# One attention block: the opening reordered, the bound's rows placed apart from Q's, and small products cut into quarters of 32 columns

## The chip, the cores and the metric

The kernel runs on one core of one Trainium2 chip. A core has five engines that each work off their own queue of instructions: TensorE (PE, matrix products), VectorE (DVE), ScalarE (ACT), GpSimd (POOL) and SyncE (SP, which here only starts DMAs). The metric is the time of one execution on the device in microseconds (us); less is better. [...]

## The reference

```python
B, S, D, H = 1, 2048, 448, 16          # Dh = 28, bf16
qkv = (x @ wqkv).reshape(B, S, 3, H, Dh).transpose(2, 0, 3, 1, 4)
q, k, v = qkv[0], qkv[1], qkv[2]
scores = einsum("bhqd,bhkd->bhqk", q, k) * Dh ** -0.5
p = softmax(scores, axis=-1)
o = einsum("bhqk,bhkd->bhqd", p, v)
out = o.transpose(0, 2, 1, 3).reshape(B, S, D) @ wo
```

It is self-attention over 2048 tokens with 16 heads of 28 channels, a projection before it and one behind it. The main work is 16 x 2048 x 2048 exponentials.

## The kernel before

**Tiling.** The 16 heads form G = 4 groups of HG = 4; each head has a strip of HP = 32 partitions, 28 of channels and four for other use. Queries come in NQC = 4 chunks of QW = 512, keys in NKT = 16 tiles of 128. A *set* is one head group and one query chunk; there are 16 sets of 4 x 16 *steps*, a step being the scores of one head, one key tile and one chunk: 128 keys x 512 queries, 1024 steps in all.

**Two ways to the exponential.** ScalarE takes two steps at a time from a pair of PSUM banks, a0 or a1, and writes exp to a tile pt (do_exp, L864, 128 x 1024). VectorE takes the other steps one by one from the banks d0, d1 and at times m: it adds a bias to the scaled scores and writes int16 whose bits, read as bf16, are a rough exponential (do_a, L879, tile I, four steps of 512 columns to a tile). Two further integer additions over the whole tile (do_add, L902, tiles J, 128 x 2048) give shifted copies. The three terms are weighted through V: VA is V, and VS holds V times two constants. So a step of VectorE is one I, half a J and three products with V, a step of ScalarE half an exponential and one product.

**Scores and P·V.** The scores of a step are one product with 32 rows (L678; 64 rows when a half of the strips is alone), and products in different row strips run together. P·V writes the 32 output columns of one head (L962), so four heads fill the four column quarters of PE together: a *wave*. The softmax sum comes from a column of ones in V. When a set ends, VectorE copies its bank (o_sb, L991), DMAs gather the sums, VectorE inverts them (L1000), DMAs spread them (L1005, L1010), and POOL multiplies (L1013).

**The bound.** In place of a row maximum, the kernel subtracts a bound: norm of the query times the largest norm of a key. It sits in spare rows of the strips, as rows of the query tiles QP against ones in K. Norms are products of squared tiles with masks (L314, L369, L449, L477); the root is a halving of the exponent bits.

**The opening.** The input is transposed by PE (L573), copied to XT by ScalarE and VectorE (L581, L579), and K of the first head group is projected and its norms taken (k_first), while Q of the first set is projected (q_job) and its norm taken (qn_first). VectorE takes the maximum of K's norms (kp, L374), multiplies the root of the bound into QA and adds Q (L463). The first scores read QA directly, 32 rows each (L678, `QA,KA`). Meanwhile SP copies QA to the tiles QP (rows_first, L613), behind 16 loads of a constant (L176); from then on scores read QP. V is projected per half of the groups and pair of key tiles (v_job, L513, full products of 224 columns) and scaled (vs_job, L532).

**What sets the order.** No engine's order is written by hand. A planner in the kernel's code runs at build time: it keeps a clock per engine (`free`), the time at which each value is there (`evt`) and each PSUM bank is free (`res`), and asks in turn each engine what it issues next (pick_pe, pick_act, pick_dve and so on). Jobs are entered with `add`, with a duration, what they need and give, the bank they take and a priority. Scores go first when their bank is free; then P·V waves, small jobs and, to keep PE in use, products of zeros (`dense`), as long as they end before the next scores are due (`s_deadline`). d_more gives VectorE a step when it would be done in time (`dve_ok`). The durations are constants:

```python
LATS = {("ACT", "PE"): 0.32, ("PE", "ACT"): 0.12, ("PE", "DVE"): 0.15, ("DVE", "PE"): 0.2}
D_S = 0.325
D_WAVE = 0.2135
D_SWITCH = 0.11
D_EXP = 0.912
SLOW_V = 1.03
```

On the chip only the order counts that comes out of this, and the semaphores between engines.

**The end.** Behind the last exponential the last set is normalised by small products instead of DMAs (L1196, L1203) and its output projected (L1213), with early parts of that projection (early_jobs, L1146) placed between (`filler`).

## Time and profile before

| | us |
|---|---|
| median of three runs | 370.25 (370.12 to 370.31) |
| the profiled execution | 370.24 |
| its span, first to last instruction | 368.4 |
| ScalarE busy, 384 instructions | 350.4 |
| of this the exponentials, L864, 368 of them | 339.2 |
| VectorE busy, 632 instructions | 347.3 |
| of this I, L879 (260 from d, 28 from m) | 170.1 and 19.0 |
| of this J, L902, 144 of them | 102.5 |
| PE busy (matmuls) | 349.5 |
| POOL busy | 72.7 |

Times in the rows below are microseconds from the start of the span. A row of a timeline gives start, length, engine, line, operation, output <- inputs, shapes, and the idle time before it with what ended it; instructions that follow each other are merged as xN. PE's matmuls overlap, so a busy PE is not a PE at its peak: the distance from start to start is what counts. The granted TensorE clock was 0.999 throughout.

### The profile page before, as it was taken

The page shows a single profiled execution, that of the slowest core. Times are in us where ns is not written, and L with a number is a line of the kernel's source. Part 1 is how long each engine was busy: PE and PEld are TensorE (multiplying, and loading weights), DVE is VectorE, ACT ScalarE, POOL GpSimd, SP SyncE. Part 2 cuts the span into 40 slices and gives each one's busy share as a digit, 9 for nine tenths or more (in the row PEclk, how much of TensorE's full clock was granted, in tenths as well). Part 3 has the DMA queues.
Part 4 walks back from the last instruction along what each step waited for, and adds up shares of the span by engine and source line. Part 5 has one row for each costly group of instructions (what it writes and reads, how often), then busy time and mean ns, then how long its engine had stood idle before and what let it go on. Part 6 is the DMA issues. An engine that isn't in the chain of part 4 may idle for free.

```text
span 368.4 us, 8926 instructions
## 1 busy us (share of the span) xinstructions
PE 349.5 (95%) x3522; PEld 111.6 (30%) x3522; DVE 347.3 (94%) x632; ACT 350.4 (95%) x384; POOL 72.7 (20%) x95
## 2 busy tenths in 40 slices
PE   8899999999999999999999999998898999999995
PEld 4443322222333233232222222222222222222222
DVE  7799999998999999999999999999999999999973
ACT  4599999999999999999999999999999999999991
POOL 8931033242010511221011314201010101010010
PEclk9999999999999999999999999999999999999999
DMA  8510010011001000010000002100000001010101
GB/s 254 126 39 12 3 29 31 8 41 36 6 29 32 2 4 28 22 52 16 29 3 9 23 4 59 24 16 18 24 8 10 25 27 55 26 56 27 42 16 50
DMA packets 15058, 12.18 MB, mean 33 GB/s; under 512 B 6812, under 2 KB 13096, under 8 KB 15016
## 3 DMA queue, kind: packets, MB, share of 16 engines
q1 hardware_dynamic: 13464, 10.19, 9.7%
q10 hardware_dynamic: 1040, 1.02, 0.9%
q8 instruction: 27, 0.44, 0.5%
q0 software_dynamic: 512, 0.40, 0.5%
q14 instruction: 15, 0.12, 0.1%
HBM read 7.58 MB, written 1.96 MB: 26 GB/s over the span
## 4 chain that ended last, share of the span: by engine, by line
PE 52%; ACT 30%; DVE 10%; issue 6%; DVEq 0%; ACTq 0%
ACT pt L864 30%; PE a L678 19%; PE o L962 16%; PE m L270 7%; DVE I L879 4%; DVE J L902 4%; PE m L547 1%; PE m L513 1%; PE o L595 1%; PE o L708 1%; PE d L678 1%; PE m L314 1%; DVE osb L552 1%; PE d L573 1%; PE a L270 1%
## 5 line engine op out<-in xcount | busy, mean ns | idle before, releaser
L864 ACT ACTIVATE pt<-a 128x1024 bf16<-128x1024 f32 x368 | 339.2, 1125 | 1.1 <-PE a L678 0.4
L879 DVE TENSOR_SCALAR I<-d 128x512 int16<-128x512 f32 x260 | 170.1, 682 | 5.3 <-PE d L678 3.9
L678 PE MATMUL a<-QP,KA 32*128 32x512 bf16 (+1 forms) x726 | 141.6, 381 | 11.2 <-ACT pt L864 10.1
L962 PE MATMUL o<-pt,VA 128*32 128x512 bf16 x736 | 105.5, 385 | 0.0
L902 DVE TENSOR_SCALAR J<-I 128x2048 int16<-128x2048 int16 x144 | 102.5, 744 | 0.2
L678 PEld LDWEIGHTS <-KA 32*128 32x128 bf16 (+1 forms) x1024 | 48.5, 91 | 145.4 <-issue 144.5
L678 PE MATMUL d<-QP,KA 32*128 32x512 bf16 x256 | 84.0, 384 | 0.4 <-DVE I L879 0.3
L962 PE MATMUL o<-J,VS 128*32 128x512 bf16 x576 | 78.7, 385 | 0.4 <-DVE J L902 0.4
L962 PE MATMUL o<-I,VA 128*32 128x512 bf16 x288 | 66.3, 386 | 0.1
L1013 POOL TENSOR_TENSOR xs<-o_sb,rr 128x512 bf16<-128x512 f32 x12 | 16.6, 1382 | 103.3 <-DMA rr<-scr 87.0
L962 PEld LDWEIGHTS <-VA 128*32 128x32 bf16 x1024 | 24.2, 94 | 36.7 <-issue 36.3
L280 POOL TENSOR_TENSOR sq<-QA 128x512 bf16<-128x512 bf16 x15 | 18.3, 1219 | 60.9 <-DVE QA L420 60.9
L270 PE MATMUL m<-XT,WRAW 112*32 112x512 bf16 x384 | 29.5, 384 | 0.0
L280 POOL TENSOR_TENSOR sq<-KA 128x512 bf16<-128x512 bf16 x12 | 13.2, 1102 | 59.2 <-DVE KA L298 59.2
L962 PEld LDWEIGHTS <-VS 128*32 128x32 bf16 x576 | 18.1, 94 | 19.7 <-issue 19.7
L879 DVE TENSOR_SCALAR I<-m 128x512 int16<-128x512 f32 x28 | 19.0, 679 | 0.1
L513 PE MATMUL m<-WRAW,XT 112*128 112x224 bf16 x128 | 17.1, 261 | 0.2
L1013 POOL TENSOR_TENSOR OTL<-o_sb,rr 128x512 bf16<-128x512 f32 x3 | 4.1, 1367 | 56.3 <-DMA rr<-scr 56.3
L708 PE MATMUL o<-zero 128*128 128x512 bf16 x40 | 13.5, 386 | 0.0
L513 PEld LDWEIGHTS <-XT 112*128 112x128 bf16 x128 | 10.2, 97 | 7.1 <-issue 7.1
L991 DVE COPY o_sb<-o 128x512 f32<-128x512 f32 x15 | 10.3, 684 | 1.4 <-PE o L962 1.3
L547 PE MATMUL m<-WO,xs 128*128 128x448 bf16 x36 | 10.9, 358 | 0.3 <-DVE I L879 0.2
(119 smaller groups left out, 195.8 us busy)
## 6 DMA issues: line engine op xcount, KB each, us to landing
rr<-scr SPq DMA_DIRECT2D x15, 256.0 KB
QP<-QA SPq DMA_DIRECT2D x60, 28.0 KB
out_dram<-osb SPq DMA_DIRECT2D x12, 112.0 KB
WRAW<-in_wqkv_dram SPq DMA_DIRECT2D x3, 392.0 KB
xs<-in_x_dram ACTq DMA_DIRECT2D x4, 224.0 KB
xs<-in_x_dram SPq DMA_DIRECT2D x4, 224.0 KB
QP<-su SPq DMA_DIRECT2D x30, 2.0 KB
out_dram<-VS SPq DMA_DIRECT2D x2, 224.0 KB
```

The lines of the kernel that those rows point to most:

```text
L270: nc.tensor.matmul(out=ps[HP * i:HP * (i + 1), :], lhsT=w[:, cc, h * Dh:h * Dh + HP], rhs=XT[c][cc // 2][:, cc % 2, :], start=(cc == 0), s ...
L280: nc.gpsimd.tensor_tensor(out=t[:], in0=src, in1=src, op=ALU.mult)
L513: nc.tensor.matmul(out=held[key][:, part * w:(part + 1) * w], lhsT=XT[b][cc // 2][:, cc % 2, t * P:(t + 1) * P], rhs=WRAW[2][:, cc, h * w: ...
L547: nc.tensor.matmul(out=held[key][:, 0:D], lhsT=otile(g, c)[:, tq * P:(tq + 1) * P], rhs=WO[:, g, :], start=(g == 0), stop=(g == G - 1))
L678: nc.tensor.matmul(out=out_ap, lhsT=KAt[(g, j // XB)][r, (j % XB) * P:(j % XB + 1) * P], rhs=q[r, :], start=True, stop=True, tile_position ...
L708: nc.tensor.matmul(out=cur["o"][:], lhsT=zero[:, 0:P], rhs=zero[:], start=False, stop=False, skip_group_check=True)
L864: nc.scalar.activation(out=pt[:], in_=ps[:], func=ACT.Exp, scale=LN2 / 128.0)
L879: nc.vector.tensor_scalar(out=dst, in0=pd[:], scalar1=BIAS, scalar2=0.0, op0=ALU.add, op1=ALU.max)
L902: nc.vector.tensor_scalar(out=r[:, w], in0=ch["I"][:, w], scalar1=float(SHIFT[k]), scalar2=None, op0=ALU.add)
L962: nc.tensor.matmul(out=o[HP * i:HP * (i + 1), :], lhsT=vt[:, j % XB, gg, HP * i:HP * (i + 1)], rhs=e["ap"], start=(SETMM[key] == 1), stop= ...
L991: nc.vector.tensor_copy(out=st["o_sb"][:], in_=o[:])
L1013: nc.gpsimd.tensor_tensor(out=otile(g, c), in0=st["o_sb"][:], in1=st["rr"][:], op=ALU.mult)
```

## The change

- **The bound of the first set.** It is no longer added to Q. Q's tile qt goes to QP by DMA as soon as it is copied (28 rows each), the bound is scaled on its own into the tile su and placed by two more DMAs. Until both have landed, scores are two products in the same bank: one of qt and one of su. The root of the query's norm is taken from PSUM on VectorE in fp32; the copy on ScalarE (L454) is gone. The margin sits in blockK.
- **The opening's banks and engines.** K's quarters and Q use other PSUM banks; two of the four copies of K (second and third quarter) are made by ScalarE; copies wait for the squares.
- **V.** It is projected for head group 0 alone, then for group 1 alone, then for groups 2 and 3 together; tiles and scalings are split alike. The gates of the later parts change.
- **Quarters.** Norm products beyond the first set, V's projection, the output projection and the zero products into an open bank are issued as four products of 32 output columns each (`quarters`).
- **The planner's costs.** D_SWITCH becomes D_TURN, charged when scores follow column work; latencies and durations change; the factor 1.03 on VectorE goes; waves are chosen one at a time.
- **The end.** The last set's scratch uses other tiles, and one filler product stands earlier.

The diff, cut to what the prediction speaks of:

```diff
-LATS = {("ACT", "PE"): 0.32, ("PE", "ACT"): 0.12, ("PE", "DVE"): 0.15, ("DVE", "PE"): 0.2}
-D_S = 0.325
-D_WAVE = 0.2135
-D_SWITCH = 0.11
-D_EXP = 0.912
-SLOW_V = 1.03
+LATS = {("ACT", "PE"): 0.165, ("PE", "ACT"): 0.167, ("PE", "DVE"): 0.13, ("DVE", "PE"): 0.145}
+D_S = 0.323
+D_TURN = 0.143
+D_WAVE = 0.226
+D_EXP = 0.904
+TOL = 0.1
...
-S_LEAD = 0.44
+S_LEAD = 0.49
...
+    def quarters(out, lhsT, rhs, start, stop, **k):
+        for i in range(P // HP):
+            r = slice(HP * i, HP * (i + 1))
+            nc.tensor.matmul(out=out[r, :], lhsT=lhsT[:, r], rhs=rhs, start=start, stop=stop, tile_position=(0, HP * i), **k)
...
-            nc.tensor.matmul(out=held[key][:, 0:QW], lhsT=maskK[:, sc, :], rhs=sqt.pop(("K", g, sc))[:],
-                             start=(sc == 0), stop=(sc == NQC - 1))
+            quarters(held[key][:, 0:QW], maskK[:, sc, :], sqt.pop(("K", g, sc))[:], sc == 0, sc == NQC - 1)
...
         def scaled():
-            held["z0"] = wk.tile([P, QW], BF16, name="z", bufs=1)
-            nc.scalar.mul(out=held["z0"][:], in_=held.pop("qn0")[:, 0:QW], mul=MARG ** 4)
...
-        def join():
-            QAt[(0, 0)] = big.tile([P, QW], BF16, name="QA0", tag="QA0", bufs=1)
-            nc.vector.scalar_tensor_tensor(out=QAt[(0, 0)][:], in0=held.pop("nq")[:], scalar=held.pop("kroot")[:, 0:1],
-                                           in1=qtt.pop(0)[:], op0=ALU.mult, op1=ALU.add)
+            su = held["su0"] = wk.tile([P, QW], BF16, name="su", bufs=1)
+            nc.vector.tensor_scalar(out=su[:], in0=held.pop("nq"), scalar1=held.pop("kroot")[:, 0:1], scalar2=None,
+                                    op0=ALU.mult)
+
+        def place():
+            for k in range(2):
+                r = slice(HP * k + Dh, P, 2 * HP)
+                nc.sync.dma_start(out=QP[0][k][0][r, :], in_=held["su0"][r, :])
...
-            q = QP[c][i % 2][g % 2] if w else QAt[(0, 0)]
...
-            nc.tensor.matmul(out=out_ap, lhsT=KAt[(g, j // XB)][r, (j % XB) * P:(j % XB + 1) * P], rhs=q[r, :],
-                             start=True, stop=True, tile_position=(r.start, 0))
+            terms = [QP[c][i % 2][g % 2]] if w else [qtt[0], held["su0"]]
+            for n, q in enumerate(terms):
+                nc.tensor.matmul(out=out_ap, lhsT=KAt[(g, j // XB)][r, (j % XB) * P:(j % XB + 1) * P], rhs=q[r, :],
+                                 start=(n == 0), stop=(n == len(terms) - 1), tile_position=(r.start, 0))
...
+            for u in range(part * n // 2, (part + 1) * n // 2):
+                for cc in range(CC):
+                    quarters(held[key][:, u * w:(u + 1) * w], XT[b][cc // 2][:, cc % 2, (t0 + u) * P:(t0 + u + 1) * P],
+                             WRAW[2][:, cc, g0 * HG * Dh:g1 * HG * Dh], cc == 0, cc == CC - 1)
...
-    k_first(1, "a1", None, "DVE", "ACT", 2.5)
-    k_first(2, "d1", "a0", "DVE", "ACT", 3.2, late=True)
-    k_first(3, "o", "m", "DVE", "ACT", 3.3, late=True)
-    q_job(0, 0, "d0", QPRI, split=1)
-    qn_first("a1", 3.5)
+    k_first(1, "a1", "o", "ACT", "ACT", 3.05, late=("ksq", 0, NQC - 1))
+    k_first(2, "d0", "a0", "ACT", "ACT", 3.1, late=("ksq", 0, NQC - 1))
+    k_first(3, "d1", "o", "DVE", "ACT", 3.2, late=("QA", 0, 0))
+    q_job(0, 0, "m", QPRI, split=1)
+    qn_first("a0", 3.3)
...
-            r = slice(HP * i, HP * (i + 1))
-            nc.sync.dma_start(out=QP[0][i % 2][0][r, :], in_=QAt[(0, 0)][r, :])
...
+            r = slice(HP * i, HP * i + Dh)
+            nc.sync.dma_start(out=QP[0][i % 2][0][r, :], in_=qtt[0][r, :])
...
+    for b in range(NXB):
+        v_job(1, b, 0, "m", 50 + b, STEPS + 10 + 12 * b)
+        vs_job(1, b, 60 + b)
+    a, z = 2 * STEPS, 2 * NQC * STEPS - 30
```

## The prediction

> **What bounds the kernel now.** I read the busy times first, then the chain of waits, the busy time of one long stretch, and the timelines of PE, DVE and POOL at single places.

> ```profile
> PE 349.5 (95%) x3522; PEld 111.6 (30%) x3522; DVE 347.3 (94%) x632; ACT 350.4 (95%) x384; POOL 72.7 (20%) x95
> ```

> Three engines are near full, so no share alone names the limit. The chain in order of time (start, length) gives ScalarE's floor:

> ```profile
> 30.80 0.76 ACT pt L864
> ...
> 31.70 0.77 ACT pt L864
> ...
> 32.61 0.78 ACT pt L864
> ...
> 33.51 0.79 ACT pt L864
> ```

> One exponential starts every 0.904 us. There are 368, the first at 19.08 and the last at 358.79: 367 steps at 0.904 are 331.8, the stretch is 339.7, so ScalarE loses 7.9. The busy time of VectorE from its first I to its last J (columns: window, length, busy):

> ```profile
> 19.96:356.70 336.74, 328.14 (x553) 1.00 0.08 24
> ```

> VectorE has only 8.6 idle in 336.7: it is nearly as full as ScalarE. Then what makes ScalarE lose. First, matmuls of unlike shape in one visit (PE timeline):

> ```profile
> 88.08 0.61 PE L962 MATMUL o<-pt,VA 128*32 128x512 bf16 x6
> 88.62 0.39 PE L477 MATMUL m<-sq,maskK 128*128 128x512 bf16 x1
> 88.94 0.39 PE L678 MATMUL a<-QP,KA 32*128 32x512 bf16 x2
> ...
> 89.27 0.39 PE L477 MATMUL m<-sq,maskK 128*128 128x512 bf16 x1
> 89.59 0.40 PE L962 MATMUL o<-J,VS 128*32 128x512 bf16 x4
> ```

> Each change between column quarters (128*32), full products (128*128) and scores (32*128) comes 0.32 after the one before; two quarter groups of one visit start 0.217 apart (150.70 and 150.93 below). A change of shape thus costs about 0.095. Here five visits fill 1.84 (88.08 to 89.92, the next scores), where two periods of ScalarE hold 1.81, and the exponential after 88.24 comes 0.29 late. Second, POOL under VectorE's J (rows of the DVE and the POOL timeline):

> ```profile
> 60.77 1.75 DVE L902 TENSOR_SCALAR J<-I 128x2048 int16<-128x2048 int16 x1
> ```

> ```profile
> 60.70 1.27 POOL L1013 TENSOR_TENSOR xs<-o_sb,rr 128x512 bf16<-128x512 f32 x1 [1.56 <-DMA rr<-scr]
> ```

> J takes 0.68 in most cases, 1.75 here. Twelve J of 144 are stretched so, 10 us in all. By start times, ScalarE has 43 gaps over 0.93; some 1.8 of its loss stand behind a stretched J, some 4.5 behind a PE that works without a pause, the rest in the first rounds.

> **The change, part by part.** Sums are made against the profiled execution, 370.24 (span 368.4 and 1.8 around it), which is the median, 370.25, within 0.01.

> *First scores.* Before, the bound is joined to Q by QA L463 (0.75) and the scores start behind it (rows of the DVE and of the PE timeline: start, length):

> ```profile
> 16.67 0.69 DVE L374 TENSOR_REDUCE kp<-m 128x1 f32<-128x512 f32 x1
> 17.28 0.28 DVE L458 TENSOR_SCALAR su<-z 128x512 int16<-128x512 int16 x1
> 17.48 0.15 DVE L378 TENSOR_REDUCE kmt<-kp 128x1 f32<-128x4 f32 x1
> 17.66 0.15 DVE L380 TENSOR_SCALAR kroot<-kmt 128x1 int32<-128x1 int32 x1
> 17.85 0.75 DVE L463 SCALAR_TENSOR_TENSOR QA<-su,kroot,qt 128x512 bf16<-128x512 bf16 x1
> ```

> ```profile
> 18.66 0.39 PE L678 MATMUL a<-QA,KA 32*128 32x512 bf16 x2 [0.32 <-DVE QA L463]
> ```

> After, the last maximum still starts near 16.6: the square of K's last quarter is still the third on ScalarE behind its projection, and that is still PE's last (moved behind one norm product). Then kmt, kroot and the scaled rows. No row has that scale (512 fp32 to bf16): between 0.21 (su's pace) and 0.60 (a copy of 512 fp32); I take 0.34, nearer the first as it reads no PSUM. The rows are ready at about 18.0. But ahead of the scores PE now makes V of a whole token block, 16 groups of four quarters of 112 columns. No row shows such a group. From below, 224 columns take 0.095 (L513 starts) and so 112 take 0.049; from above, fp32 quarters of 128 columns take 0.46 for 16, so 0.115 for four:

> ```profile
> 362.38 0.64 PE L1203 MATMUL a<-identf,rT 128*32 128x128 f32 x16
> 362.84 0.62 PE L1203 MATMUL o<-identf,rT 128*32 128x128 f32 x16
> ```

> I take 0.065, near the lower end, because bf16 quarters keep the pace of a full product (0.217 for 512). V then ends near 17.55, a filler and the first q product follow, and the first bound product starts at 18.18. The exponential needs 0.64 more (a second pair of slots, then 0.42 as from 18.66 to 19.08): 18.8 for 19.08, a gain of 0.3.

> *Rounds two to six.* Until the query rows are placed by DMA, each score is two products in the same 32 rows, the second behind the first. A round of three scores holds four slots of 0.217, for one or two before. PE's order has, from the second round to the seventh: 19 score slots (4.12), ten changes of shape (0.95), three fillers and one wave of P·V (0.87), four V halves of eight groups (2.08 at 0.065): 8.0, and 0.65 from the first bound product to round two. The seventh exponential, the first from placed rows, starts at 18.18 + 0.65 + 8.0 + 0.42 = 27.2; before, the seventh starts at 25.36 (two rows of 0.904 behind 23.55). **+1.9** with the first gain inside. By 0.049 per group it is +1.2, by 0.115 +4.3. Nothing hides it: ScalarE has no other work there, and one V copy left on it for three (0.41 each) lies ahead of the first exponential.

> *The rows' DMAs.* That Q's rows go alone lets them start when Q is copied (near 15.8), but SP works off the 16 loads of offs until then:

> ```profile
> 7.37 11.10 SPq L176 DMA_DIRECT2D QP<-offs  x16
> 18.63 2.48 SPq L613 DMA_DIRECT2D QP<-QA  x4
> ```

> They start at 18.5 as before, now four of 28 rows (0.82 apart at L425) and two of the bound (0.59 apart): issued by 22.5, landed by about 24.1 (1.6 behind the issue, as the packets of L613). PE comes to the first wide round at 26.8, so they cost nothing; behind them SP has only the next Q's rows, due after 30.

> *Two exponentials fewer.* The planner now gives 366 to ScalarE and 292 half steps to VectorE (before 288): 2 x 0.904 = **-1.8**.

> *Quarters and the planner's new costs.* Pricing each group in PE's order by 0.217 for 512 columns and 0.095 for a change of shape, the part of a round above 0.904, summed over rounds 24 to 345, falls from 4.2 to 2.9 (741 changes of shape become 685 over all). The 4.5 that ScalarE loses to a busy PE fall by the same share: **-1.5**. Bounds: nothing, and -3.0 if short overfull rounds are caught by the buffers.

> *VectorE.* It gains four I (0.60 each), two J (0.60), two V copies (0.53) and 0.15 of scales in smaller pieces: 4.8, priced by pace from start to start. KA of two quarters goes to ScalarE before its first exponential, where it waits anyway. By order, VectorE's work per 23 exponentials (20.8 of ScalarE) is 17.8 to 21.5 in the last third before, but 20.9, 21.2, 21.1, 20.9, 21.4 after; with 0.8 per stretch for stretched J and slow I (13 us over 16 stretches) each is above 20.8. The worst run of stretches stands 3.1 above ScalarE before and 5.5 after: **+2.4**. Bounds: 0 if all 4.8 go into the 8.6 idle, +4.8 if none do. Which J POOL meets will shift too, since POOL starts when its DMA lands: 12 now, and the row gives no sign.

> *Tail.* Six exponentials follow VectorE's last scores in both, the closing products keep their order but for one filler: 0, within 0.2.

> Sum: 370.2 + 1.9 - 1.8 - 1.5 + 2.4 = **371.2**.

> **Rivals.** *VectorE's idle time takes the added work* (faster). Half its idle stands behind a crowded PE (3.9 waiting for d), and that is what shrinks. If no VectorE loss is added and PE's relief is -3.0: 370.2 + 1.9 - 1.8 - 3.0 = 367.3. It decides as soon as VectorE's idle in the long stretch falls below about 4. For it: ScalarE's loss is mostly PE's. Against it: the five full stretches in the last third.

> *Groups of 112 columns take 0.115* (slower still): 371.2 + 2.4 = 373.6; decided in the first seven exponentials. For it, only the fp32 rows. [...]

> *The double products don't cost a slot each.* If PE overlaps the two of one row group, the opening ends with the rows' landing, 24.1, and the seventh exponential starts near 25.4: 369.3. Against it: before, a second score in the same rows starts 0.217 behind the first (18.66 and 18.89).

> *All terms cancel*: 370.2.

> **Chances and range.** Forecast (opening lost, VectorE fuller) 0.40, its own range 370.8 to 373; 0.115 per group 0.08; cancelled 0.13; VectorE hides it 0.31; cheap double products 0.08. 0.2% (0.74 us) is about what can be told from no change. Slower 0.48, same 0.13, faster 0.39. The range runs from 366.5 (the first rival and 0.8 for fewer stretched J) to 375.0 (0.115 and more of the 4.8).

> **What would show it.** Right: first exponential near 18.8, seventh near 27.2; 366 exponentials; VectorE idle below 6 in its long stretch; few gaps of ScalarE behind a PE without pause, more behind d that waits for I. Wrong: a seventh exponential before 26; ScalarE's loss behind the seventh under 5; J stretched far less or more than 10 us in all.

## The result and the profile after

The changed kernel takes 368.74 us (368.31 to 368.86, five runs), the kernel before on the same chip 370.18 (369.90 to 370.31, five): ratio 0.9954, 95% interval 0.9940 to 0.9968. It is 1.2 to 2.2 us faster where 371.2 was predicted; the range (366.5 to 375.0) holds it, the sign is wrong. The profiled execution took 368.69, its span is 366.9, the granted clock was 1.0.

The busy times of the page after, and VectorE's long stretch (columns: window, length, then busy time of PE, its weight loads, VectorE, ScalarE and POOL, granted clock, DMA share, GB/s):

```profile
PE 345.5 (94%) x4528; PEld 112.3 (31%) x4529; DVE 347.6 (95%) x646; ACT 348.9 (95%) x381; POOL 70.8 (19%) x103
```

```profile
19.20:356.21 337.01, 321.34 (x4187) 100.17 (x4186) 329.27 (x567) 334.47 (x364) 53.21 (x52) 1.00 0.09 25
```

VectorE is busy 0.3 us longer than before over the whole span and 1.1 longer in this stretch (329.27 for 328.14), where it is idle for 7.7 of 337.0; the forecast asked for less than 6. The pace of ScalarE is again 0.904. The start times of the exponentials split the span:

| | before | after | predicted for after |
|---|---|---|---|
| first exponential | 19.08 | 18.86 | 18.8 |
| seventh | 25.37 | 25.22 | 27.2 |
| lost in the first six steps | 0.87 | 0.94 | about 3.0 |
| exponentials | 368 | 366 | 366 |
| lost behind the seventh | 7.1 | 8.2 | 8.0 |
| last exponential's start to the end | 9.63 | 8.97 | 9.6 |

The span changed by -0.22 (first exponential), +0.07, -1.81 (two steps fewer), +1.11 and -0.66: -1.5. The first term is no property of the change: two executions of the changed kernel have it at 18.86 and 19.60, because x lands at different times (the first 16 transposes of x take 1.06 and 1.91 us). From the last maximum of K's norms (kp) to the first exponential it is 2.41 before (16.67 to 19.08) and 2.29 and 2.28 after: 0.12 of gain, where 0.3 was forecast.

The opening, in PE's timeline of the changed kernel (start, length):

```profile
16.46 0.97 PE L289 MATMUL m<-WRAW,XT 112*32 112x112 bf16 x64
...
20.03 0.39 PE L699 MATMUL a<-qt,KA 32*128 32x512 bf16 x2
20.04 0.38 PE L699 MATMUL d<-qt,KA 32*128 32x512 bf16 x1
20.25 0.38 PE L699 MATMUL a<-su,KA 32*128 32x512 bf16 x2
20.27 0.37 PE L699 MATMUL d<-su,KA 32*128 32x512 bf16 x1
...
23.87 0.38 PE L699 MATMUL a<-su,KA 32*128 32x512 bf16 x2
23.89 0.37 PE L699 MATMUL d<-su,KA 32*128 32x512 bf16 x1
24.19 0.58 PE L289 MATMUL m<-WRAW,XT 112*32 112x112 bf16 x32
24.70 0.39 PE L699 MATMUL a<-QP,KA 32*128 32x512 bf16 x2
```

The program issues qt, su, qt, su, qt, su. The three of qt start together and the three of su 0.22 behind them: a round of double products takes two slots, not four. The 64 quarter products of V's 112 columns start within 0.8 us: 0.049 for a group of four. The first round that reads placed rows starts at 24.70, 6.5 behind the first product of the bound; 8.65 was predicted. SP issued those rows as foreseen, and their last packets start at 23.58, 1.1 ahead of that round:

```profile
18.51 3.22 SPq L631 DMA_DIRECT2D QP<-qt  x4
21.83 1.09 SPq L478 DMA_DIRECT2D QP<-su  x2
```

The closing stage:

```profile
359.61 0.37 PE L289 MATMUL a<-WO,xs 128*32 128x448 bf16 x2
359.93 0.61 PE L1214 MATMUL a<-self__165,V 128*128 128x4 f32 x4
360.39 0.59 PE L1214 MATMUL o<-self__165,V 128*128 128x4 f32 x4
360.91 0.65 PE L1220 MATMUL a<-identf,rT 128*32 128x128 f32 x16
```

From the products of self to those of identf 0.52 pass for 0.92 before: of the two fillers that stood between (a<-WO,xs, 361.91 in the trace of before), one is now done beside the last waves and one behind the products of identf.

### The profile page after: what moved, and what is told of

The parts are those of the page before. It is cut to its first block, busy times and chain, and to the rows that moved or that the text cites. A ratio compares the mean times of both kernels' runs of the same rounds, so it can differ in the third digit from the quotient of the medians.

```text
span 366.9 us, 10993 instructions
## 1 busy us (share of the span) xinstructions
PE 345.5 (94%) x4528; PEld 112.3 (31%) x4529; DVE 347.6 (95%) x646; ACT 348.9 (95%) x381; POOL 70.8 (19%) x103
## 4 chain that ended last, share of the span: by engine, by line
PE 34%; ACT 30%; DVE 27%; issue 7%; DMA 1%; DVEq 0%; ACTq 0%
ACT pt L891 30%; DVE I L906 12%; PE a L699 12%; PE o L987 9%; DVE J L929 7%; PE m L289 4%; PE m L282 4%; DVE QP L180 1%; DVE V L540 1%; DVE QA L436 1%; DVE KA L315 1%; DVE z L495 1%; PE d L699 1%; DVE o_sb L1016 1%; DVE V L552 1%
## 5 line engine op out<-in xcount | busy, mean ns | idle before, releaser
L987 PE MATMUL o<-pt,V 128*32 128x512 bf16 x732 | 104.2, 384 | 0.0
L929 DVE TENSOR_SCALAR J<-I 128x2048 int16<-128x2048 int16 x146 | 101.8, 724 | 0.3
L699 PE MATMUL d<-QP,KA 32*128 32x512 bf16 (+1 forms) x258 | 83.3, 383 | 1.3 <-DVE I L906 1.3
L987 PE MATMUL o<-J,V 128*32 128x512 bf16 x584 | 76.6, 384 | 0.4 <-DVE J L929 0.3
L987 PE MATMUL o<-I,V 128*32 128x512 bf16 x292 | 68.6, 384 | 0.7 <-DVE o_sb L1016 0.5
L987 PEld LDWEIGHTS <-V 128*32 128x32 bf16 x1608 | 28.6, 94 | 49.6 <-issue 47.0
L289 PE MATMUL m<-WRAW,XT 112*32 112x112 bf16 (+1 forms) x768 | 18.1, 230 | 0.2 <-DVE V L540 0.2
L289 PEld LDWEIGHTS <-XT 112*32 112x32 bf16 x768 | 11.7, 96 | 10.3 <-issue 10.1
L289 PE MATMUL m<-WO,xs 128*32 128x448 bf16 x156 | 12.5, 359 | 0.0
L436 DVE CAST QA<-m 128x512 bf16<-128x512 f32 x15 | 10.2, 683 | 1.1 <-PE m L282 0.5
L699 PE MATMUL m<-QP,KA 32*128 32x512 bf16 x29 | 11.1, 384 | 0.0
L289 PE MATMUL m<-sq,maskK 128*32 128x512 bf16 x108 | 10.8, 388 | 0.1
```

The source lines that it names most:

```text
L289: nc.tensor.matmul(out=out[r, :], lhsT=lhsT[:, r], rhs=rhs, start=start, stop=stop, tile_position=(0, HP * i), **k)
L436: nc.vector.tensor_copy(out=t[:], in_=held[key][:, 0:QW])
L699: nc.tensor.matmul(out=out_ap, lhsT=KAt[(g, j // XB)][r, (j % XB) * P:(j % XB + 1) * P], rhs=q[r, :], start=(n == 0), stop=(n == len(terms ...
L929: nc.vector.tensor_scalar(out=r[:, w], in0=ch["I"][:, w], scalar1=float(SHIFT[k]), scalar2=None, op0=ALU.add)
L987: nc.tensor.matmul(out=o[HP * i:HP * (i + 1), :], lhsT=VT[e["k"]][g, j // XB][:, j % XB, HP * i:HP * (i + 1)], rhs=e["ap"], start=(SETMM[k ...
```

## The experiments

Every ratio below is to the kernel before, run on the same chip.

**Are strips independent of program order?** A kernel of zero products alone (the attention is left out) issues three row strips with two products each as A A B B C C and as A B C A B C, the same for four column strips, then A A B, then groups of four quarters of 112 and of 28 columns.

```python
for n in range(4):
    for i in (0, 1, 2):
        for k in range(2):      # and with the two inner loops exchanged
            nc.tensor.matmul(out=bank[i][:], lhsT=zero[r, 0:P], rhs=zero[r, :], start=(k == 0), stop=(k == 1), tile_position=(32 * i, 0))
```

> Leaves out the whole computation: PE works on zeros and the output is zeros. Blocks of products: (1) three row strips, each with two products that follow each other in the program (A A B B C C), four times; (2) the same as A B C A B C; (3) and (4) the same with the four column quarters of 128 x 32; (5) strip A twice, then strip B once, eight times; (6) 64 groups of four quarters with 112 columns; (7) the same with 28 columns. Theory: each strip works off its own products and does not wait for the program's order, so block 1 takes as long as block 2, two slots of 0.217 for six products, 1.74 us for 24. Rival: products start in the program's order, and only a product of a busy strip waits; then block 1 takes 4 slots for its first six, and about 3.5 us in all against 1.74 for block 2. [...]

Its PE timeline, the two row orders, the two column orders, and the start of A A B (L75 is A, L77 is B):

```profile
8.22 1.91 PE L52 MATMUL b<-zero 32*128 32x512 bf16 x24
...
10.60 1.90 PE L58 MATMUL b<-zero 32*128 32x512 bf16 x24
...
12.97 1.92 PE L64 MATMUL colb<-zero 128*32 128x512 bf16 x32
...
15.36 1.91 PE L70 MATMUL colb<-zero 128*32 128x512 bf16 x32
...
17.74 0.38 PE L75 MATMUL b<-zero 32*128 32x512 bf16 x1
17.74 0.39 PE L77 MATMUL b<-zero 32*128 32x512 bf16 x1
17.96 0.37 PE L75 MATMUL b<-zero 32*128 32x512 bf16 x1
17.97 0.37 PE L77 MATMUL b<-zero 32*128 32x512 bf16 x1
```

All four orders take the same 1.9 us, eight steps of 0.216. In the last rows B, third in the program, starts beside the first A, and the second B (sixth) beside the second A: each strip works off its own products and runs ahead of the others. Between strips, then, these products do not start in program order, and the rival's 3.5 us for the first order was not seen. Groups of 112 columns start 0.049 apart, of 28 columns 0.025, and the four quarters of a group within 0.01 of each other: the four strips do not take turns.

**What does the opening cost?** The changed kernel with the bound again added to Q and one product per first score, in the same planned order:

```diff
-            nc.vector.tensor_scalar(out=su[:], in0=held.pop("nq"), scalar1=held.pop("kroot")[:, 0:1], scalar2=None, op0=ALU.mult)
+            nc.vector.scalar_tensor_tensor(out=su[:], in0=held.pop("nq"), scalar=held.pop("kroot")[:, 0:1], in1=qtt[0][:], op0=ALU.mult, op1=ALU.add)
...
-            terms = [QP[c][i % 2][g % 2]] if w else [qtt[0], held["su0"]]
+            terms = [QP[c][i % 2][g % 2]] if w else [held["su0"]]
```

> The changed kernel, in which the first set's bound is again added to Q on VectorE, so that each of the first scores is one product; the planned order is the same. Theory (a pair of products costs one slot of 0.217 in a round, and PE is what the first rounds wait for): the scaled rows come 0.27 later (0.67 for 0.40), the first exponential needs one slot less, so it starts within 0.1 of 18.86; five further rounds are shorter by 0.217 each, ScalarE gains some 0.5 to 1.0 by its seventh exponential: 367.7 to 368.2 for 368.7. Rival (the opening is hidden behind VectorE's work or behind the landing of the placed rows): 368.7 within 0.3.

Measured 368.51 (367.07 to 372.50, 12 runs), ratio 0.9974 (0.9948 to 1.0000). The spread has a cause that its profiled execution (370.55) shows, in PE's timeline and in the stretches behind it:

```profile
24.87 0.39 PE L699 MATMUL a<-QP,KA 32*128 32x512 bf16 x1 [0.94 <-DMA QP<-su]
25.82 0.37 PE L699 MATMUL a<-QP,KA 32*128 32x512 bf16 x1 [0.56 <-DMA QP<-qt]
```

```profile
24.00:26.00 2.00, 0.56 (x3) 0.27 (x3) 1.29 (x3) 0.52 (x1) 0.00 (x0) 1.00 0.02 3
26.00:28.00 2.00, 2.00 (x28) 0.50 (x30) 1.69 (x4) 1.77 (x2) 0.00 (x0) 0.94 0.00 0
28.00:30.00 2.00, 2.00 (x19) 0.32 (x18) 1.65 (x3) 1.52 (x3) 0.18 (x1) 0.50 0.00 0
30.00:32.00 2.00, 2.00 (x58) 0.82 (x53) 1.22 (x3) 1.45 (x2) 1.23 (x1) 0.71 0.06 14
```

PE reaches the placed rows earlier than they land, stands for 1.5 us, and 2 us later its granted clock (the third column from the right) is at 0.50. In eight of the twelve runs the mean clock is 0.997 or more and the span 365.3 to 366.9; in four it is 0.991 to 0.995 and the span 367.1 to 370.7.

So the rows were moved ahead: of the 16 loads of offs on SP's queue, two stay in front and 14 follow the first rows.

```diff
-    for z in range(2):
-        for c in range(NQC):
-            for k in range(2):
-                nc.sync.dma_start(out=QP[c][k][z][...], in_=offs[:])
+    offset_rows(0, 0)          # two loads; the other 14 behind the two DMAs of place()
```

> The kernel with the bound joined to Q and one product per first score, in which two of the sixteen loads of offs stay ahead of the first rows on SP's queue and fourteen go behind them. Theory, a late landing of the rows stops PE and then the granted clock falls: the rows start near 15.8 us for 19.9, PE waits for no DMA between 20 and 30 us, the granted clock is 0.997 or more in every run, all runs lie within 1 us, and the median is 0.7 to 1.2 us below the changed kernel (the seventh exponential at 24.3 to 24.6 us). Rival, the clock falls because a single product per score leaves PE too little work: a third of the runs stay at 0.991 to 0.995 with 369 to 372 us.

> The changed kernel itself, as the measure for the three kernels beside it. Both theories: 0.9954 of the time before, within 0.0015; one exponential each 0.904 us, the seventh near 25.2 us, the first round that reads the placed rows about 1 us behind their landing, so that PE does not wait for them and its granted clock stays at 0.997 or more in every run.

Early rows: 368.70 (367.64 to 369.79, 11 runs), ratio 0.9961 (0.9948 to 0.9973). The changed kernel beside it: 368.77 (367.56 to 369.71, 12 runs), 0.9966 (0.9953 to 0.9980). The cause is confirmed: no run has a clock under 0.997, and the first six steps lose 0.04 for 0.94. The gain is not: the medians agree within 0.1, though the profiled spans (366.9 and 367.9) differ as expected. The changed kernel's profiled execution is its slowest of twelve, and the first exponential of the changed and the joined kernels lies anywhere from 18.86 to 19.60, so one pair of spans says little. The two intervals leave room for a gain of 0.9 at the most; where it goes is open.

**What do quarters give?** The changed order with full products in place of quarters:

```diff
-            quarters(held[key][:, 0:QW], maskK[:, sc, :], sqt.pop(("K", g, sc))[:], sc == 0, sc == NQC - 1)
+            nc.tensor.matmul(out=held[key][:, 0:QW], lhsT=maskK[:, sc, :], rhs=sqt.pop(("K", g, sc))[:], start=(sc == 0), stop=(sc == NQC - 1))
```

and so at every other call.

> The changed kernel with every product that it cuts into quarters issued as one full product, in the same planned order. Theory (a change of shape costs 0.095, and a crowded PE is most of what ScalarE loses): changes of shape rise from 685 to 727, the part of rounds above 0.904 by 2.2 us, in the tail two changes come back: 370.4 to 371.4 for 368.7. Rival (the quarters are worth nothing, the two exponentials fewer and the opening are all): 368.7 within 0.4.

Measured 369.44 (368.92 to 371.06, 12 runs), ratio 0.9989 (0.9974 to 1.0004): by the ratios 0.9 us above the changed kernel, between the theory's 1.7 and the rival's 0.4, the intervals overlapping by a little. The profiled execution is the slowest of the twelve. It loses 9.8 behind the seventh (8.2 and 8.4 in two executions of the changed kernel) and has a closing stage of 9.18 (8.97). It also loses 1.45 in the first six steps (0.94), but that is not the full products: here the placed rows landed late, and PE stood for the DMA of su's rows at 25.32.

**The moved filler.**

```diff
-    filler(3)
+    filler(2)
...
+    filler(2)
     for hf in range(2):
         for k in range(2):
             for i in range(HG):
```

> The changed kernel with the fillers of the closing stage where they stood before: two ahead of the transposes and two between the reciprocals and the products of identf and rT, for three and none. Theory, the moved fillers are 0.4 of the closing stage's 0.67: from the last exponential's start to the end of the span 9.35 us for 8.95, and 0.3 to 0.5 us slower than the changed kernel. Rival, the fillers lie beside other work and the stage is shorter for its quarter products alone: 8.95 and no difference.

Measured 369.32 (368.15 to 371.26, 12 runs), 0.55 above the changed kernel beside it; from the last exponential to the end 9.45 us for 8.97. The rows of its closing stage:

```profile
360.88 0.59 PE L1214 MATMUL o<-self__165,V 128*128 128x4 f32 x4
361.40 0.56 PE L289 MATMUL a<-WO,xs 128*32 128x448 bf16 x8
361.79 0.61 PE L1221 MATMUL a<-identf,rT 128*32 128x128 f32 x16
```

The eight quarters stand on the path again. The theory holds: the fillers are 0.5 of the stage's 0.66; by full, the quarters are the other 0.2.

**Quarters alone, in the kernel before.** The same replacement, the other way round, in the kernel before and its order:

> The kernel before with its small products (norms of later sets, V, output projection, zero products into an open bank) cut into quarters of 32 columns, in its own planned order. Theory: changes of shape fall from 741 to 700, the part of rounds above 0.904 from 8.7 to 6.2 us, so 367.5 to 368.3 for 370.2, all of the whole change's gain or more. Rival (quarters are worth nothing by themselves): 370.2 within 0.4.

Measured 371.92 (370.50 to 373.55, 8 runs), ratio 1.0063 (1.0039 to 1.0087): slower, which no theory had. Seven runs had a clock of 0.988 to 0.995; the profiled one (370.50) had 1.0. Since late rows had lowered the clock in the opening, the loads of offs were moved here too:

> The kernel before with its small products in quarters, and two of the sixteen loads of offs ahead of the first rows, fourteen behind them. Theory, quarters alone were slow because the first rows landed late, PE paused and the granted clock fell to 0.988 to 0.995 in seven runs of eight: the clock is 0.997 or more in every run, no wait of PE for the rows, and the time is 0.3 to 1.5 us below the kernel before. Rival, the quarters themselves lower the clock or crowd PE: 371 to 373 us and the same low clocks.

Measured 372.52 (370.48 to 374.46, 9 runs), eight of nine with 0.989 to 0.995: that theory falls. This profile, though, caught the place. PE's timeline, and the stretches from 60 us on:

```profile
61.03 0.39 PE L685 MATMUL a<-QP,KA 32*128 32x512 bf16 x2
63.48 0.39 PE L685 MATMUL d<-QP,KA 32*128 32x512 bf16 x1 [2.06 <-DMA QP<-su]
```

```profile
62.00:64.00 2.00, 0.52 (x5) 0.21 (x9) 0.10 (x1) 0.81 (x1) 0.67 (x1) 1.00 0.09 33
64.00:66.00 2.00, 2.00 (x22) 0.33 (x14) 1.91 (x3) 1.02 (x1) 1.14 (x2) 0.69 0.00 0
66.00:68.00 2.00, 2.00 (x17) 0.39 (x16) 1.29 (x2) 1.20 (x2) 0.50 (x1) 0.50 0.00 0
```

The next chunk's rows of the bound are late. SP's queue tells why, in the kernel before and then with quarters (loads not moved):

```profile
54.08 0.47 SPq L1005 DMA_DIRECT2D scr<-rec  x1
55.63 0.60 SPq L1010 DMA_DIRECT2D rr<-scr  x1
56.32 2.10 SPq L493 DMA_DIRECT2D QP<-su  x4
```

```profile
54.44 0.47 SPq L1006 DMA_DIRECT2D scr<-rec  x1
57.52 0.60 SPq L1011 DMA_DIRECT2D rr<-scr  x1
58.22 2.09 SPq L496 DMA_DIRECT2D QP<-su  x4
```

rr reads what scr wrote, so SP waits for that write to land: 1.55 us before, 3.1 and (early loads) 3.5 with quarters. The rows of the bound stand behind rr in the queue. The packets of scr with quarters, from the trace's DMA records:

```
start   took   bytes  queue
55.497  0.932  16384  instruction
55.601  0.011     64  data (120 such packets since 55.41)
56.414  0.028     64  data (the last eight, to 56.51)
```

The last packets start when a 16 KB transfer of the instruction queue ends; with early loads they do so at 57.02, behind a transfer from 55.70 to 57.04. That is 0.8 and 1.2 of the delay. From the last packet to the issue of rr pass another 1.0 us, for 0.4 before, and what holds SP there is not shown. The kernel before has such transfers at 50.58 and 62.22 and none between. Quarters raise PE's products from 3522 to 4299 and these transfers from 27 to 33, so they fall elsewhere. Over this trace 4299 products and as many weight loads on 33 transfers are 260 to one; in the traces before and after, 254 on average start between one transfer and the next (210 to 289 and 187 to 317). To test whether this meeting makes the quarters slow, the ten warming products at the start became forty short ones, 60 instructions more:

```diff
-    for _ in range(10):
-        nc.tensor.matmul(out=warm[:], lhsT=zero[:, 0:P], rhs=zero[:], start=True, stop=True)
+    for n in range(40):
+        q = slice(n % 4 * P, (n % 4 + 1) * P)
+        nc.tensor.matmul(out=warm[:, q], lhsT=zero[:, 0:P], rhs=zero[:, q], start=True, stop=True)
```

> The kernel before with its small products in quarters, and the ten warming products of 512 columns at the start made as forty of 128: the same columns, 60 instructions more on PE. In the two runs of these quarters a 16 KB transfer of the instruction queue started at 55.50 and 55.70 us, amid the write of scr (rec), whose last packets came behind it; the next DMA on SP, rr from scr, and the rows of the bound behind that in SP's queue came 1.9 us late, PE stood 1.4 to 2.1 us and its granted clock fell. Theory, that meeting made the quarters slow: with some 256 instructions in a transfer and 11 us between two, 60 instructions move it to about 53 us; then rr is issued within 1.8 us of scr, PE waits for no DMA near 61 us, the clock is 0.997 or more in nearly all runs, and the time is 368.5 to 370.3. Rival, the quarters themselves: 371.5 to 372.5 and 0.988 to 0.995 as before.

> The changed kernel with the same forty warming products of 128 columns, so that the instruction transfers come some 2 to 3 us earlier. Theory, the gain of the change does not hang on where these transfers fall: within 0.5 us of the changed kernel (0.996 to 0.9975 of before). Rival, the gain is luck of their places: 1 us slower or more, with a DMA wait of PE and a lower clock in the records.

Measured 369.46 (368.10 to 370.70, 12 runs), ratio 0.9978 (0.9964 to 0.9991), eleven of twelve clocks at 0.999 or more; the transfer now starts at 52.91:

```profile
55.65 0.47 SPq L1007 DMA_DIRECT2D scr<-rec  x1
57.20 0.61 SPq L1012 DMA_DIRECT2D rr<-scr  x1
57.90 2.09 SPq L496 DMA_DIRECT2D QP<-su  x4
```

Sixty instructions more in the first 6 us take 2.5 us off the time (3.1 by the ratios), at 61 us. The forecast that PE would wait for nothing there was too good: it still stands 0.77, and the clock stays at 1.0. (The rows go out at 57.90 for 58.22, but this execution's first exponential came 0.74 later; against it they are 1.1 earlier.) So quarters alone, in the order before and with the transfer out of the way, are worth 0.8 us (0.3 to 1.3), where 1.9 to 2.7 were expected.

The changed kernel with the same shift: 368.70 (368.15 to 369.73, 10 runs), 0.9965 (0.9951 to 0.9979), so its gain does not hang on these places. But its profiled execution shows the DMA wait that the rival named. The 16 loads of offs took 13.0 us in place of 11.3, the first rows went out late,

```profile
20.74 3.22 SPq L632 DMA_DIRECT2D QP<-qt  x4
```

PE stood for them around 26 us, the seventh exponential came at 27.01, and 2.1 us were lost in the first six steps, with the clock at 1.0. Late rows are no matter of the shift: of nine profiled executions with the changed opening, five lose 0.94 there and four lose 1.17, 1.31, 1.45 and 2.09, all four with PE waiting for the rows.

**What does VectorE's work cost?** The squares and most of the normalisation are left out: POOL makes no squares and multiplies 8 of 512 columns; the order of all engines is the same:

```diff
-        t = new_sq(key)
-        nc.gpsimd.tensor_tensor(out=t[:], in0=src, in1=src, op=ALU.mult)
+        sqt[key] = src
...
-            nc.gpsimd.tensor_tensor(out=otile(g, c), in0=st["o_sb"][:], in1=st["rr"][:], op=ALU.mult)
+            nc.gpsimd.tensor_tensor(out=otile(g, c)[:, 0:8], in0=st["o_sb"][:, 0:8], in1=st["rr"][:, 0:8], op=ALU.mult)
```

> The changed kernel in which POOL makes no squares (K and Q are fed unsquared to the norm products of the later groups) and multiplies 8 of the 512 columns by the reciprocals: the squares and most of the normalisation are left out, the order of all engines is the same. J is then stretched by less than 1 us in all for 7.0. Theory, VectorE sets the loss of ScalarE behind the seventh exponential (8.2 us) as the prediction priced it, half of each us of VectorE's work: 2.5 to 4 us faster than the changed kernel. Rival, a crowded PE sets it: 0 to 1 us faster.

> The kernel before with the same left out (squares of the later groups, 504 of 512 columns of the normalisation). J is stretched by less than 1 us in all for 10.2. Theory of the prediction (before, 1.8 us of the loss stand behind stretched J, the rest behind PE): 1.5 to 2.5 us faster than the kernel before. Rival, VectorE sets the loss here too, half of each us: 4 to 5 us faster. Rival, it costs nothing: within 0.5.

The group of J in the changed kernel, and with light POOL (busy, mean ns | idle before):

```profile
L929 DVE TENSOR_SCALAR J<-I 128x2048 int16<-128x2048 int16 x146 | 101.8, 724 | 0.3
```

```profile
L930 DVE TENSOR_SCALAR J<-I 128x2048 int16<-128x2048 int16 x146 | 95.7, 682 | 0.3
```

No J is stretched any more: 6.1 us less for VectorE. The changed kernel gains 1.5 (367.38; ratio 0.9925 for 0.9966), the kernel before 1.3 (368.63; 0.9964) from 8.7 less (102.5 to 93.8). A microsecond of VectorE is worth 0.25 and 0.15, not 0.5. The first run lies between the theory's 2.5 and the rival's 1, the second just below the theory's 1.5.

The other way, the factor 1.03 on VectorE is given back to the planner of the changed kernel:

```diff
-        self.eng, self.dur, self.emit = eng, dur, emit
+        self.eng, self.dur, self.emit = eng, dur * (1.03 if eng == "DVE" else 1.0), emit
```

and in the durations of I and J.

> The changed kernel whose planner again counts VectorE's durations 1.03 times: four exponentials more (370), eight half steps of VectorE fewer (284) and four J fewer, some 7.2 us less work for VectorE. Theory of the prediction (half of VectorE's added work comes back as ScalarE's loss): 3.6 for the exponentials less 3.6 of loss, within 1 us of the changed kernel. Rival, VectorE's work is hidden: 3 to 4 us slower. Rival, all of it is paid: 3 us faster or more.

Measured 370.32 (369.31 to 370.72, 10 runs), ratio 0.9998 (0.9986 to 1.0011): 1.2 slower. Of the 3.6 for four more exponentials 2.4 came back, for 4.4 less of VectorE's busy time (343.2) or 7.2 by count. Other durations also give another order, so not all of the 2.4 is VectorE's work: some 0.9 of it is a wait for a DMA that this order does not have (the last paragraph of this section). The other 1.5 make 0.35 for a microsecond. Trading exponentials for VectorE's steps pays, as the change did it.

**A better plan.** POOL's multiplication starts some 10 us behind o_sb (9.4 to 15.3 in the changed kernel), where the plan has 11.3:

```diff
-        add("SP", 0.5, spread, need=[("scr", s)], gives=[("rr", s)], land=5.5, pri=2)
+        add("SP", 0.5, spread, need=[("scr", s)], gives=[("rr", s)], land=4.6, pri=2)
```

> The changed kernel whose planner expects the spread of the reciprocals 0.9 us earlier (4.6 for 5.5), since POOL's multiplication starts about 10.4 us behind the copy o_sb where the plan has 11.3; the planner keeps J out of the time in which it expects POOL at work. Theory, stretched J come from plan and chip differing here: at most 4 stretched J for 8, 3 to 4 us less of VectorE, 1 to 2 us faster than the changed kernel. Rival, the landing scatters by more than 0.9 (10.1 to 16 us in the changed kernel) and J is met as often: within 0.7 us.

> The changed kernel with the reciprocals' landing planned 0.9 us earlier, again with more rounds, since four runs gave 0.994 of before (0.9917 to 0.9963): 0.9935 to 0.995 if its shorter loss of ScalarE behind the seventh exponential (6.7 for 8.2 to 8.4 us) is the order's; 0.9965 as the changed kernel if it was one execution's chance.

> The earlier landing in the plan, the bound joined to Q with one product per first score, and fourteen of the sixteen loads of offs behind the first rows. Theory, the opening's loss of 0.9 and the loss behind it add: ScalarE loses 0.1 us in the first seven exponentials and about 6.7 behind them, 366.7 to 367.2 us. Rival, what the opening gains is given back behind it (the joined kernel with early rows was no faster than the changed kernel by its median): 367.5 to 367.9.

Measured 367.77 (367.43 to 368.36, 4 runs), ratio 0.9940 (0.9917 to 0.9963), and again 367.93 (367.59 to 369.09, 6 runs), 0.9947 (0.9928 to 0.9967). Together with the joined bound and early rows: 367.93 (367.01 to 368.62, 6 runs), 0.9938 (0.9920 to 0.9956). These are the fastest kernels here that compute the whole, 2.1 us below the kernel before and some 0.8 below the changed one, though the intervals overlap that of the changed kernel. The opening's 0.9 is lost a second time.

That fewer stretched J make the gain is not shown. The theory had at most four of them. J's group is 98.6 and 99.0 with six and five stretched J in the first two, but 101.0 with seven in the third, which is as fast; the changed order itself has 100.1 to 101.8 with six to eight in seven executions. The loss behind the seventh, 6.7 in the first profiled execution, is 8.0 and 7.6 in the others (the second is the slowest of its six runs). What in the order gains is open.

**Where the loss behind the seventh stands.** The kept traces can say it. Each distance between two exponentials, less 0.904, is sorted by whether PE stands still for 0.1 us or more within it, and for which engine (us; small excesses under 0.03 are in the rest):

| | before | changed | changed again | full | before, quarters, shifted |
|---|---|---|---|---|---|
| PE never stands | 4.5 | 3.8 | 4.0 | 4.6 | 2.7 |
| PE stands for VectorE | 1.4 | 2.7 | 2.8 | 3.2 | 1.4 |
| of this at the wait for den, below | 0 | 0.9 | 1.0 | 1.2 | 0 |
| the rest | 1.2 | 1.7 | 1.6 | 2.0 | 2.4 |
| sum | 7.1 | 8.2 | 8.4 | 9.8 | 6.5 |

So quarters do relieve a crowded PE: 4.5 to 2.7 in the order before (where the rest holds 1.1 at the late rows of the bound), 4.6 to 3.8 or 4.0 in the changed one. The changed order does not crowd PE more (4.6 for 4.5 without quarters); it makes PE wait more for VectorE, most of it at one place:

```profile
87.34 6.84 SPq L441 DMA_DIRECT2D QP<-QA  x8
94.29 0.60 SPq L1021 DMA_DIRECT2D den<-o_sb  x1
96.20 0.25 DVE L1025 RECIPROCAL rec<-den 128x16 f32<-128x16 f32 x1 [1.09 <-DMA den<-o_sb]
```

The copy o_sb ends at 91.13, but the DMA that gathers its sums (den) stands on SP's queue behind rows of Q and goes out at 94.29. The reciprocal (rec) stands in VectorE's queue ahead of the next I, so VectorE is idle for 1.09 us with work behind it, PE waits for the bank of that I, and the exponential at 98.34 comes 0.94 late. In the kernel before den goes out at 91.80, 0.03 behind o_sb, and VectorE does not wait. Wait and loss go together over all eight executions of the changed plan, joined, full and with light POOL included: 0.66 and 0.50, 0.74 and 0.59, 1.05 and 0.89, 1.09 and 0.94, 1.14 and 0.99, 1.20 and 0.98, 1.31 and 1.16, 1.39 and 1.21. The three kernels with the earlier landing in the plan wait 1.40 to 1.74 there and lose 1.20 to 1.45; the kernel before, in all its forms, and the slow costs have neither. No run moved den alone.

## Why the prediction was wrong

By its own steps, in us of the span:

| step | predicted | measured |
|---|---|---|
| First scores, rounds two to six | +1.9 | -0.15 (+0.07 without the first exponential's chance) |
| The rows' DMAs | 0 | 0 here, by 1.1 us of room; 0.2 to 1.2 in four other executions |
| Two exponentials fewer | -1.8 | -1.81 |
| Quarters and the planner's new costs | -1.5 | -0.66 (PE never stands: 4.47 to 3.81) |
| VectorE | +2.4 | +0.31 (PE stands for VectorE, without den) |
| The wait for den | not in the sum | +0.94 |
| Other small losses behind the seventh | not in the sum | +0.52 |
| Tail | 0 | -0.66 |

- **Rounds two to six** is the step that gave the wrong sign. It put both products of a score one behind the other in PE as a whole, "four slots of 0.217"; the strips overlap, and a round has two. That is 1.7 of the 2.2 us between 8.65 and 6.5; the other 0.5 are groups of 112 columns at 0.049, the lower bound, in place of 0.065. The rival on cheap double products had it, at 0.08. The argument against it, a second score in the same rows 0.217 behind the first, was true and no argument: it speaks of one strip. With -0.15 in place of +1.9 the prediction's own sum would have been 369.2, faster than before.
- **Tail** counted the closing products and overlooked that the moved filler stood on the path. It measured 0.5, and quarters 0.2.
- **Quarters** had the right mechanism, a PE relieved of changes of shape, and half the size here. In the order before they take 1.8 off this loss, about what was said, but the late rows of the bound take 1.1 back and the time fell by 0.8. The pace of 0.217 that the price of a change of shape was taken from stands in PE's timeline of before, between two groups of four quarters:

```profile
150.70 0.39 PE L962 MATMUL o<-J,VS 128*32 128x512 bf16 x1
150.70 0.39 PE L962 MATMUL o<-pt,VA 128*32 128x512 bf16 x1
150.71 0.39 PE L962 MATMUL o<-J,VS 128*32 128x512 bf16 x1
150.71 0.39 PE L962 MATMUL o<-pt,VA 128*32 128x512 bf16 x1
150.93 0.39 PE L962 MATMUL o<-J,VS 128*32 128x512 bf16 x2
```

- **VectorE** was priced by count: 4.8 more. By busy time it is 1.1 and 0.5 more in the long stretch of two executions, partly since eight and seven J are stretched for twelve; and a microsecond costs 0.15 to 0.35 (light POOL, slow costs), not 0.5.
- **The wait for den** is a term that the prediction did not have. It looked at SP's queue for the first rows only ("behind them SP has only the next Q's rows, due after 30") and not at what the new order puts ahead of later transfers. That the steps on quarters and VectorE, +0.9 together, came near the measured +1.1 behind the seventh is therefore cancellation.
- Right were the two exponentials and that stretched J would change in a way the row gave no sign of. The rows' landing was right in this execution, with less room than others needed. The first exponential met its 18.8 by luck: 18.86 to 19.60 in nine executions.

## What to carry to other kernels

Count PE's time by strip, not by program order: in all four orders tried here, products in other strips filled the gaps (1.90 to 1.92 us each). Look at what stands on one DMA queue ahead of a transfer with little room (den went out 3.16 us behind o_sb), and at what stands behind the instruction that waits for it; in two of the traces here a late landing cost PE waits of 1.5 and 2.06 us and a clock of 0.50 behind them. When a loss is what remains of a sum, sort it by who waited in the trace before giving it a cause. And when a change adds many small instructions, compare where the instruction transfers fall before blaming the instructions.

## What was not expected of the hardware

- **An instruction transfer met data.** One 16 KB transfer of 0.93 us held up eight packets of 64 bytes by 0.8 us, and with that a chain of three DMAs. The transfer stood at the same place in both traces of the order before with quarters (55.50 and 55.70); 15 of these 17 runs had a lower clock, and with 60 instructions more one of twelve.
- **Short groups stopped with no operand missing.** In the kernel of zero products, 64 groups of 28 columns:

```profile
27.52 0.55 PE L87 MATMUL colb<-zero 128*32 128x28 bf16 x51
29.39 1.19 PE L87 MATMUL colb<-zero 128*32 128x28 bf16 x128 [1.32 <-issue]
33.39 0.80 PE L87 MATMUL colb<-zero 128*32 128x28 bf16 x77 [2.81 <-issue]
```

At 0.025 a group they would take 1.6 us; they take 6.5, with PE waiting for no operand, and instruction transfers start at 27.01 and 31.04. The groups of 112 columns before them stop once too, for 1.67 us. That the instructions came too slowly is the author's estimate from these times; no run changes their supply.
